# Channel attention and GELU feed-forward on one Trainium2 core: vector and scalar work in a written order, and a plain first step in each pair

## Chip, core and metric

The kernel runs on one core of a Trainium2 chip. TensorE (PE) multiplies, VectorE (DVE) and ScalarE (ACT) empty PSUM and do the elementwise work, SyncE (SP) issues the transfers. Every engine works through its own instruction stream and waits at semaphores for the others. The metric is the device time of one execution in microseconds (us); lower is better.

## What is computed

```python
B, N, C = 4, 6080, 256                          # q, k, v: (B, N, C); w_in (256, 2048), w_out (2048, 256)
qn = q / (norm(q, axis=1) + 1e-6)               # norms over the N positions of each channel
kn = k / (norm(k, axis=1) + 1e-6)
a = softmax(kn.transpose(0, 2, 1) @ qn / tau)   # 256 x 256 for each batch
x = (v @ a).reshape(24320, 256)
out = gelu(x @ w_in) @ w_out                    # exact gelu, with erf
```

## The kernel before

The attention matrix is folded into the first weight: `(v @ a) @ w_in` is `v @ (a @ w_in)`, so each batch has its own first-layer weight, which `w_part` makes in four groups `g` of 512 columns. Operands of products are kept as a high and a low fp32r half, and one product is three matmuls (high*high, high*low, low*high; `passes`).

Work is cut by batch `b` (4), by pair `p` (6 pairs of two chunks of 512 positions; the last pair, p=5, has two of 480) and by step `u` (8 steps, each with two of the sixteen 128-row blocks of the hidden layer): 192 steps in all, `steps`. A step does the first layer of its own blocks (`first_products`) and, between these, the second layer of the step before it (`second_products`, a generator that is advanced once or twice after each first-layer product). The first layer is a Strassen-Winograd scheme of seven products in the order of `ORDER`; they run in two PSUM banks, which the program calls `h` (`one` and `two` in the code, taken from a `ring`). Product 0 in `one` is copied out to SBUF by ACT (`p1`), product 1 in `two` likewise (`p5`), product 2 is accumulated in `one` and copied (`u2`); later products are added to these copies by DVE (`added`, L572), and GELU follows on ACT (L525, L526 for the high half and the whole, `whole` L535 where the scheme also covers the second layer).

Where `strassen(b, p, u)` holds, the second layer of the step also uses the scheme: four full products of 512 columns for the chunk j=1 and seven of 256 columns for chunk j=0 (into the PSUM tiles c00, c01, p0, p1), whose operands `sums` makes on DVE and ACT (x, then casts into gh1/gl1 of 768 columns, L552/L557, and gh0/gl0 of 1024, L556/L558; in the last pair 720 and 960). Where it does not, the second layer is eight full products. At the end of a pair `combine` and `merge` add p0, p1 and c00, c01 together and the result is stored.

Beside this, while batch b runs, the kernel prepares batch b+1 (`extras`): it loads tiles of q and k (`load_qk`), splits them into high and low (`split_qk`, L199 on ACT, L200 on DVE), multiplies them in bursts of eight matmuls in an `h` bank (`burst`) and adds the result to `sacc` on DVE (L218); it loads transposed tiles (raw<-kqt) and squares them on ACT for the norms (`norm_part`, L226); in the steps 36 and after of the batch it does the softmax and, from step 41, makes the next weights: `w_part` multiplies six times into an `h` bank, ACT scales the result out (hl, L437), DVE forms four sums and ACT and DVE split them into wh and wl. The values of v for the next pair are split in the last step of each pair (`v_split`, L494 and L495).

The order of instructions on each engine comes from a scheduler that orders by its own estimates of time. Only PE's instructions are held in the order in which the program writes them, from the point where "filled" is set (at the end of the first attention matrix):

```python
def pe(op, *args, **kw):
    r = op(*args, **kw)
    if "filled" in state:
        tc.keep_in_program_order(r)
    return r
```

The pair (0, 0) uses the plain form of the first layer as well (`plain_products`) while the second weight is still being narrowed from fp64; in the pair (0, 1) `sum_wo` forms the scheme's sums of the second weight once and stores them.

Of the kernel before, what the change touches and what calls it, by code (L numbers as in the profile page):

```python
# [60 lines left out]
def channel_attention_gelu_ffn(ctx, tc, qk, kqt, vt, tau, w_in, w_out, out):  # L61
# [62 lines left out]
    def pe(op, *args, **kw):  # L124
        r = op(*args, **kw)  # L125
        if "filled" in state:
            tc.keep_in_program_order(r)
        return r

    def mm(*args, **kw):  # L130
        return pe(nc.tensor.matmul, *args, **kw)
# [41 lines left out]
    def qk_fill():  # L173
        state["fill"] = s = psum("c00").rearrange("p (m c) -> p m c", m=NCT)
        for i in range(FILL * JS):
            js, j = divmod(i, JS)
            raw = raws[1, js]
            for m in range(NCT):
                marks["fill"] = nc.tensor.matmul(
# [16 lines left out]
    def split_qk(b, js):  # L196
        raw = raws.pop((b, js))
        hl = pqk.tile([P, 2, JS, 2, C], F32R, name="hl", bufs=3)
        nc.scalar.copy(out=hl[:, 0], in_=raw)  # L199
        nc.vector.tensor_tensor(out=hl[:, 1], in0=raw, in1=f32(hl[:, 0]), op=ALU.subtract)  # L200
        hls[b, js] = hl


    def burst(b, k, m):
# [7 lines left out]
        if k == 0:  # L212
            if m == 0:
                state["sacc"] = pm.tile([P, NCT, NT], F32, name="sacc")
            nc.vector.tensor_copy(out=state["sacc"][:, m], in_=s)
        else:
            acc = state["sacc"][:, m]
            nc.vector.tensor_tensor(out=acc, in0=s, in1=acc, op=ALU.add)  # L218

    def norm_part(b, t, c):  # L220
# [5 lines left out]
        nc.scalar.activation(out=x, in_=x, func=AF.Square, accum_out=state["nsum"][:, t, c:c + 1])  # L226
# [8 lines left out]
    def narrow(hi, lo, raw):  # L235
# [12 lines left out]
        nc.vector.tensor_scalar(out=top, in0=high.bitcast(F32), scalar1=TOP_MAX, scalar2=-TOP_MAX,  # L248
                                op0=ALU.min, op1=ALU.max)
        nc.scalar.activation(out=tail, in_=top, func=AF.Square)  # L250

        topu = top.bitcast(U32)
        nc.vector.tensor_scalar(out=body, in0=topu, scalar1=0x07FFFFFF, scalar2=3,
                                op0=ALU.bitwise_and, op1=ALU.logical_shift_left)
        nc.vector.scalar_tensor_tensor(out=topu, in0=topu, scalar=0xC0000000, in1=body,
                                       op0=ALU.bitwise_and, op1=ALU.bitwise_or)
        nc.vector.scalar_tensor_tensor(out=w, in0=tail, scalar=TOP_MIN ** 2, in1=top, op0=ALU.is_ge, op1=ALU.mult)

        body = high
        nc.vector.tensor_scalar(out=body, in0=w.bitcast(U32), scalar1=0xFF800000, scalar2=None, op0=ALU.bitwise_and)  # L260
        nc.vector.scalar_tensor_tensor(out=tail, in0=low, scalar=2.0 ** -52, in1=body.bitcast(F32), op0=ALU.mult,
                                       op1=ALU.mult)
        nc.scalar.copy(out=hi, in_=w)
        nc.vector.tensor_tensor(out=w, in0=w, in1=f32(hi), op=ALU.subtract)
        nc.vector.tensor_tensor(out=lo, in0=w, in1=tail, op=ALU.add)
# [30 lines left out]
    def sum_wo(u):  # L296
# [6 lines left out]
        tt = nc.vector.tensor_tensor  # L303
        tt(out=full, in0=f32(wo[:, 0]), in1=f32(wo[:, 1]), op=ALU.add)
# [3 lines left out]
        tt(out=s4, in0=a12, in1=s2, op=ALU.subtract)  # L308
        new_ws((0, 1, u))
        ws = wss.pop((0, 1, u))  # L310
        hi, lo = (ws[:, i].rearrange("p s c -> p (s c)") for i in range(2))
        nc.scalar.copy(out=hi, in_=x[:, 1])
# [4 lines left out]
    def preload(func, after):  # L317

        junk = pm.tile([P, 16], F32, name="junk")
        nc.scalar.activation(out=junk[:, 0:2], in_=after.bitcast(F32)[:, 0:2], func=func)  # L320

    def softmax(first):
# [5 lines left out]
        for m in range(NCT):  # L328
            t = pm.tile([P, C], F32, name=f"t{m}")
            if first:  # L330
                nc.scalar.copy(out=t, in_=state["s"][m])
            else:
                s = state["sacc"]
                nc.vector.tensor_tensor(out=t, in0=s[:, m, 0:C], in1=s[:, m, C:2 * C], op=ALU.add)
            ts.append(t)
        nsum = state.pop("nsum")
        if first:
# [4 lines left out]
            nc.vector.reduce_sum(out=z, in_=nsum[:, :, NSQ // NSJ:NSC], axis=AX.X)  # L342
            nc.vector.tensor_tensor(out=x, in0=nps[:, 0:2 * NCT], in1=z, op=ALU.add)
        else:
            nc.vector.reduce_sum(out=x, in_=nsum[:, :, 0:NSC], axis=AX.X)
        nc.vector.tensor_scalar(out=x, in0=x, scalar1=1e-30, scalar2=None, op0=ALU.max)
        yield

        nc.scalar.activation(out=y, in_=x, func=AF.Sqrt)
        if first:  # L350
            preload(AF.Exp, y)
        nc.vector.reciprocal(out=z, in_=y)
        nc.vector.tensor_tensor(out=z, in0=z, in1=x, op=ALU.mult)
        nc.vector.scalar_tensor_tensor(out=z, in0=z, scalar=2e-6, in1=y, op0=ALU.add, op1=ALU.add)
        nc.vector.reciprocal(out=r, in_=z)

        diag = pm.tile([P, NCT, P], F32, name="diag")
        nc.vector.tensor_tensor(out=diag, in0=ident.unsqueeze(1).broadcast_to([P, NCT, P]),
                                in1=r[:, NCT:2 * NCT].unsqueeze(2).broadcast_to([P, NCT, P]), op=ALU.mult)
        nc.vector.tensor_scalar(out=rk, in0=r[:, 0:NCT], scalar1=rtau, scalar2=4.0, op0=ALU.mult, op1=ALU.mult)  # L360
# [3 lines left out]
        for m in range(NCT):  # L364
            nc.vector.scalar_tensor_tensor(out=ts[m], in0=ts[m], scalar=rk[:, m:m + 1], in1=rq[:, 0:C],
                                           op0=ALU.mult, op1=ALU.mult)
            nc.vector.reduce_max(out=nms[:, m:m + 1], in_=ts[m], axis=AX.X, negate=True)
# [56 lines left out]
    def w_part(b, g, m):  # L424
# [19 lines left out]
        if m == 0:  # L444
            return
# [514 lines left out]
```

## Time and profile before

| | |
|---|---|
| median of 3 runs | 2304.08 us (2302.96 to 2306.28) |
| the profiled execution | 2306.74 us, its span 2305.0 us |
| mean granted TensorE clock | 0.987 |
| busy: PE, DVE, ACT | 2188.7, 1746.6, 1639.4 us |

Rows are read thus. A group of instructions has its source line, engine, operation, tiles (out<-in), shape and count, then its busy time and the mean time of one in ns, then the idle time of the engine ahead of it and what ended that. A wait row names who waited for whom: total us, times, longest. A row of a timeline has start and duration in us, and in brackets the idle time before it. A row of windows has, for a stretch of the execution, the busy time of each engine with its number of instructions, then the mean granted clock of TensorE and the DMA share. PE's busy time runs on while its last matmul drains.

### The profile page before, as it was taken

How to read it: one execution, taken by the hardware profiler on the slowest of the kernel's cores; microseconds unless marked ns; L12 is line 12 of the kernel's file. 1: busy time of each engine (PE TensorE's matmuls, PEld its weight loads, DVE VectorE, ACT ScalarE, POOL GpSimd, SP SyncE). 2: the span in 40 equal slices, each digit the busy share in tenths (PEclk: the TensorE clock that was granted, in tenths of full speed). 3: DMA queues.
4: the chain of work that ended last, by engine and by line, in shares of the span. 5: the costliest groups of instructions: out<-in, count | busy, mean ns of one | idle time of the engine just before them, and what ended most of it. 6: DMA issues, size and time to landing. Idle time of an engine off the chain costs nothing.

```text
span 2305.0 us, 30506 instructions
## 1 busy us (share of the span) xinstructions
PE 2188.7 (95%) x11239; PEld 1838.8 (80%) x11239; DVE 1746.6 (76%) x2777; ACT 1639.4 (71%) x2702; POOL 1.3 (0%) x8
## 2 busy tenths in 40 slices
PE   9899999998899999999889999999988999999998
PEld 7687788887777887788777787778877788888886
DVE  6987778877677787887767778788676787787774
ACT  6667777767567777776766777777666677777664
POOL 0000000000000000000000000000000000000000
PEclk9999999999999999999999999999999999999999
DMA  9446555434235555543324555553342332433331
GB/s 380 168 149 226 191 183 201 171 120 146 110 136 198 176 201 174 190 157 119 146 110 149 190 174 200 175 191 127 110 146 110 127 136 103 147 145 119 119 120 71
DMA packets 103429, 363.74 MB, mean 158 GB/s; under 512 B 10608, under 2 KB 12656, under 8 KB 101232
## 3 DMA queue, kind: packets, MB, share of 16 engines
q1 hardware_dynamic: 103280, 361.80, 44.3%
q8 instruction: 88, 1.44, 0.3%
q14 instruction: 61, 0.50, 0.1%
HBM read 324.27 MB, written 37.49 MB: 157 GB/s over the span
## 4 chain that ended last, share of the span: by engine, by line
PE 59%; DVE 14%; ACT 14%; DMA 8%; issue 5%; ACTq 0%; SPq 0%; DVEq 0%
PE h L125 29%; PE c L125 21%; PE p L125 7%; DMA raw<-kqt 7%; DVE h L572 3%; ACT x L535 3%; ACT raw L226 2%; DVE gl L557 2%; ACT gh L525 2%; PE h L167 2%; ACT gh L556 2%; DVE hl L200 2%; ACT g L526 2%; DVE x L549 2%; DVE gl L558 1%
## 5 line engine op out<-in xcount | busy, mean ns | idle before, releaser
L125 PE MATMUL c<-gh,wo 128*128 128x512 f32 (+3 forms) x2372 | 840.0, 362 | 0.0
L125 PE MATMUL h<-vh,wh 128*128 128x512 f32 (+1 forms) x1312 | 533.8, 407 | 99.6 <-ACT hl L437 48.8
L125 PE MATMUL h<-vl,wh 128*128 128x512 f32 (+1 forms) x1312 | 519.3, 396 | 0.0
L125 PE MATMUL h<-vh,wl 128*128 128x512 f32 (+1 forms) x1312 | 518.7, 395 | 0.0
L125 PEld LDWEIGHTS c<-gh,wo 128*128 128x128 f32 x2372 | 451.6, 190 | 76.2
L525 ACT ACTIVATE gh<-h 128x512 fp32r<-128x512 f32 (+1 forms) x402 | 250.4, 623 | 265.3 <-DVE h L572 246.9
L125 PE MATMUL c<-gl,wo 128*128 128x512 f32 (+3 forms) x1186 | 425.4, 359 | 0.0
L125 PEld LDWEIGHTS h<-vh,wh 128*128 128x128 f32 x1312 | 249.7, 190 | 183.1 <-ACT hl L437 58.5
L527 DVE TENSOR_TENSOR gl<-g,gh 128x512 fp32r<-128x512 f32 (+1 forms) x418 | 284.6, 681 | 82.6 <-ACT g L526 80.0
L558 DVE TENSOR_TENSOR gl<-x,gh 128x1024 fp32r<-128x1024 f32 (+1 forms) x175 | 211.9, 1211 | 138.3 <-ACT gh L556 138.3
L572 DVE TENSOR_TENSOR h<-h,p 128x512 f32<-128x512 f32 (+1 forms) x368 | 249.9, 681 | 64.5 <-PE h L125 56.0
L125 PEld LDWEIGHTS h<-vh,wl 128*128 128x128 f32 x1312 | 249.8, 190 | 53.7
L125 PEld LDWEIGHTS h<-vl,wh 128*128 128x128 f32 x1312 | 250.1, 191 | 31.0 <-DVE vl L495 0.3
L567 ACT COPY p<-h 128x512 f32<-128x512 f32 (+1 forms) x368 | 211.4, 580 | 80.8 <-PE h L125 80.5
L125 PEld LDWEIGHTS c<-gl,wo 128*128 128x128 f32 x1186 | 225.5, 190 | 43.1
L535 ACT ACTIVATE x<-h 128x512 f32<-128x512 f32 (+1 forms) x350 | 200.2, 603 | 65.2 <-DVE h L572 59.0
L526 ACT ACTIVATE g<-h 128x512 f32<-128x512 f32 (+1 forms) x402 | 245.2, 610 | 1.4 <-DVE h L572 1.4
L125 PE MATMUL p<-gh,ws 128*128 128x256 f32 (+1 forms) x1050 | 240.4, 280 | 0.0
L556 ACT CAST gh<-x 128x1024 fp32r<-128x1024 f32 (+1 forms) x175 | 181.8, 1039 | 78.2 <-DVE x L555 77.2
L572 DVE TENSOR_TENSOR h<-h,u 128x512 f32<-128x512 f32 (+1 forms) x184 | 125.6, 683 | 110.5 <-PE h L125 109.2
L125 PEld LDWEIGHTS p<-gh,ws 128*128 128x128 f32 x1050 | 185.9, 189 | 7.8
L549 DVE TENSOR_TENSOR x<-x 128x512 f32<-128x512 f32 (+1 forms) x175 | 119.7, 684 | 94.8 <-ACT x L535 94.5
(176 smaller groups left out, 2777.7 us busy)
## 6 DMA issues: line engine op xcount, KB each, us to landing
wo<-keep_out SPq DMA_DIRECT2D x184, 512.0 KB, 4.5
ws<-keep_sum SPq DMA_DIRECT2D x175, 512.0 KB, 3.6
raw<-qk SPq DMA_DIRECT2D x95, 512.0 KB, 4.5
raw<-kqt SPq DMA_DIRECT2D x72, 512.0 KB, 4.3
v_raw<-vt SPq DMA_DIRECT2D x20, 1024.0 KB, 6.2
out<-osb SPq DMA_DIRECT2D x40, 512.0 KB, 2.8
hl<-keep_in SPq DMA_DIRECT2D x12, 1024.0 KB, 7.4
raw<-w_in SPq DMA_DIRECT2D x8, 512.0 KB, 6.9
```

Source lines behind the costliest of these rows:

```text
L125: r = op(*args, **kw)
L167: marks["scores"] = nc.tensor.matmul(s[m], raw[:, j, 0, m * P:(m + 1) * P], raw[:, j, 1], start=(js == 0 and j == 0), stop=(js * JS + j == ...
L200: nc.vector.tensor_tensor(out=hl[:, 1], in0=raw, in1=f32(hl[:, 0]), op=ALU.subtract)
L525: nc.scalar.activation(out=gh[:, :n], in_=src, func=AF.Gelu)
L526: nc.scalar.activation(out=g[:, :n], in_=src, func=AF.Gelu)
L527: nc.vector.tensor_tensor(out=gl[:, :n], in0=g[:, :n], in1=f32(gh[:, :n]), op=ALU.subtract)
L535: nc.scalar.activation(out=state["x"][:, at:at + n], in_=src, func=AF.Gelu)
L549: tt(out=x[:, 4 * h:6 * h].rearrange("p (k c) -> p k c", k=2), in0=x[:, h:3 * h].rearrange("p (k c) -> p k c", k=2), in1=x[:, 0:h].unsquee ...
L556: nc.scalar.copy(out=ht[:, :4 * h], in_=x[:, 4 * h:8 * h])
L558: tt(out=lt[:, :4 * h], in0=x[:, 4 * h:8 * h], in1=f32(ht[:, :4 * h]), op=ALU.subtract)
L567: nc.scalar.copy(out=t[:, :n], in_=ps[:, :n])
L572: nc.vector.tensor_tensor(out=h[:, :n], in0=ps[:, :n], in1=t[:, :n], op=ALU.add)
```

## The change

Three things change.

1. From the pair (0, 1) on ("pinned"), the instructions of DVE and ACT are held in the order of the program, as PE's are. In the first pair (0, 0) PE's instructions are now left to the scheduler too.
2. The program is written slot by slot: the seven first-layer products of a step are its slots 0 to 6, `EDGE` (8) is its end. Splits, sums, squares, `v_split`, `combine`, `merge` and the softmax are cut into parts, and a table of jobs puts each part at a step and slot. The low half of a gelu is issued behind the next DVE eviction (`pending`, `flush`).
3. `strassen` is false for u=0 in every pair: the second layer of that step takes eight full products. The bursts of batches 2 and 3 come every 2.8 steps from step 4 (before: every 3 from step 2).

```diff
+    class InOrder:
...
+            def issue(*args, **kw):
+                r = op(*args, **kw)
+                if "pinned" in state:
+                    tc.keep_in_program_order(r)
+                return r
...
+    pe, dve, act = InOrder(nc.tensor), InOrder(nc.vector), InOrder(nc.scalar)
...
     def strassen(b, p, u):
-        return p > 1 if b == 0 else (b, p, u) != (B - 1, NP - 1, NU - 1)
+        return u > 0 and (b, p) > (0, 1) and (b, p, u) != (B - 1, NP - 1, NU - 1)
...
+    def flush():
+        for x in pending:
+            x()
+        pending.clear()
...
-        nc.vector.tensor_tensor(out=gl[:, :n], in0=g[:, :n], in1=f32(gh[:, :n]), op=ALU.subtract)
+        act.activation(out=gh[:, :n], in_=src, func=AF.Gelu)
+        act.activation(out=g[:, :n], in_=src, func=AF.Gelu)
+        pending.append(lambda: dve.tensor_tensor(out=gl[:, :n], in0=g[:, :n], in1=f32(gh[:, :n]), op=ALU.subtract))
...
     def sums(n):
...
-        nc.scalar.copy(out=hb[:, :3 * h], in_=x[:, h:4 * h])
-        yield
+        act.copy(out=hb[:, :3 * h], in_=x[:, h:4 * h])
         tt(out=t2, in0=t3, in1=b11, op=ALU.add)
+        yield
         tt(out=t4, in0=b21, in1=t2, op=ALU.subtract)
-        nc.scalar.copy(out=ht[:, :4 * h], in_=x[:, 4 * h:8 * h])
+        yield
+        act.copy(out=ht[:, :4 * h], in_=x[:, 4 * h:8 * h])
         tt(out=lb[:, :3 * h], in0=x[:, h:4 * h], in1=f32(hb[:, :3 * h]), op=ALU.subtract)
+        yield
         tt(out=lt[:, :4 * h], in0=x[:, 4 * h:8 * h], in1=f32(ht[:, :4 * h]), op=ALU.subtract)
...
+    def spread(gen, step, *slots):
+        for x in slots:
+            at(step + x // 10, x % 10, lambda: next(gen, None))
...
+            def split(b=b, js=js, step=prev + 1 + t):
+                gen = split_qk(b, js)
+                next(gen)
+                at(step, 2, lambda: next(gen, None))
+            at(prev + 1 + t, 1, split)
...
+            def norm(b=b, i=i, step=base + 8 + i):
+                gen = norm_part(b, *divmod(i, NSC))
+                with behind("kept"):
+                    next(gen)
+                at(step + 1, 2, lambda: next(gen, None))
+            at(base + 8 + i, EDGE, norm)
+        def soft(step=base + 36):
+            gen = softmax(False)
+            next(gen)
+            spread(gen, step, 10, 12, 10 + EDGE, 20, 23, 20 + EDGE)
...
+                spread(w_split(b, g), step, 10, 11, 12, 20, 22, 23)
...
+                    def end(b=b, p=p, step=base + NU + 1):
+                        gen = combine(b, p)
+                        next(gen)
+                        spread(gen, step, 1)
+                        for c in range(NCT):
+                            at(step, 2, lambda c=c: merge(b, p, c))
...
+        if (b, p) == (0, 1):
+            spread(sum_wo(u), i, 0, 1, 3, 4)
...
+        for slot, _ in enumerate((plain_products if plain else first_products)(b, p, u)):
+            for _ in range(1 if slot < 4 or count < 11 else 2):
+                next(second, None)
+            if slot < 2:
+                next(rest, None)
+            run(i, slot)
...
+        if mine:
+            rest = sums(PAIRS[p][1])
+            next(rest)
...
+        run(i, EDGE)
+        run(i, EDGE + 1)
+        if mine:
+            next(rest)
```

Three places show what moves. The changed kernel's DVE and ACT instructions all stand under the line of `issue`, L133.

ACT in the fourth step of the last pair of batch 0 (b=0, p=5, u=3), from the cast of the 720 columns to u2; before:

```order
L552 CAST gh_5475<-x 128x720
L556 CAST gh_5477<-x 128x960
L437 ACTIVATE hl<-h_5494,rden 128x512
L567 COPY p_5519<-h_5515 128x480
L397 CAST wh_78<-hl 128x768
L567 COPY p_5528<-h_5524 128x480
```

and now:

```order
L133 CAST gh_5428<-x 128x720
L133 ACTIVATE hl<-h_5439,rden 128x512
L133 COPY p_5452<-h_5448 128x480
L133 CAST gh_5430<-x 128x960
L133 CAST wh_78<-hl 128x768
L133 COPY p_5464<-h_5460 128x480
```

The cast of 960 columns stood ahead of the scaled eviction `hl` and of the copy p1; it now stands behind both.

ACT in a step of 512 columns with a square for the norms (b=1, p=2, u=4), before:

```order
L552 CAST gh_8416<-x 128x768
L567 COPY p_8447<-h_8443 128x512
L226 ACTIVATE raw,nsum<-raw 128x1024
L567 COPY p_8456<-h_8452 128x512
L556 CAST gh_8418<-x 128x1024
L567 COPY u_8464<-h_8443 128x512
```

and now, to the first gelu of the step:

```order
L133 COPY p_8352<-h_8348 128x512
L133 CAST gh_8324<-x 128x1024
L133 COPY p_8363<-h_8359 128x512
L133 CAST hl<-raw 128x1024
L133 COPY u_8374<-h_8348 128x512
L133 ACTIVATE raw,nsum<-raw 128x1024
L133 ACTIVATE gh<-h 128x512
```

The square of the loaded tile stood between the copies p1 and p5; it now stands behind u2, and one cast of `split_qk` between p5 and u2.

DVE in the pair (0, 1), from the last gelu halves of one step to the first eviction of the next (x<-wo is the first sum of `sum_wo`, which reads a loaded weight), before:

```order
L527 TENSOR_TENSOR gl_1711<-g,gh_1710 128x512
L527 TENSOR_TENSOR gl_1723<-g,gh_1722 128x512
L304 TENSOR_TENSOR x<-wo 128x512
L572 TENSOR_TENSOR h<-h_1762,u_1774 128x512
L305 TENSOR_TENSOR x<-x 128x128
```

and now:

```order
L133 TENSOR_TENSOR gl_1719<-g,gh_1718 128x512
L133 TENSOR_TENSOR gl_1731<-g,gh_1730 128x512
L133 TENSOR_TENSOR x<-wo 128x512
L133 TENSOR_TENSOR x<-x 128x128 x4
L133 TENSOR_TENSOR hl<-raw,hl 128x1024
L133 TENSOR_TENSOR h<-h_1759,u_1777 128x512
```

The four small sums, and in such a step the low half of a split, came behind the eviction of `two`; they now stand ahead of it.

More of the change, by code (lines that the diff above doesn't have):

```diff
@@ L605, in first_products @@
         do(6, one, False, True)
+        flush()
         chunk0(one[:, :n], 0)
         later(name)
-        if strassen(b, p, u):
-            state["sums"] = sums(n)
-            next(state["sums"])
     def plain_products(b, p, u):
@@ L641, in second_products @@
         mine = strassen(b, p, u)
-        if u == 0:
-            po.clear()
-            po["mixed"] = any(strassen(b, p, x) for x in range(NU))
-            po["plain"] = not all(strassen(b, p, x) for x in range(NU))
+        po = pos.setdefault((b, p), {})
+        mixed = any(strassen(b, p, x) for x in range(NU))
         def acc(name):
@@ L705, in second_products, with store @@
             passes(o[:, half * h:(half + 1) * h], *w, hi[:, k * h:(k + 1) * h], lo[:, k * h:(k + 1) * h], first, last)
-            if name == "c01":
-                if last:
-                    combine(b, p)
-                    if u == NU - 1:
-                        merge(b, p, 0)
-                        merge(b, p, 1)
-                        store(0, po["y"])
-            yield
+            if last and name == "c01" and u < NU - 1:
+                for _ in combine(b, p):
+                    pass
+            yield
+    def store(b, p, j, osb):
+        t0, n = PAIRS[p]
+        t = b * N + t0 + j * n
+        dst = out[:, t:t + n].rearrange("(t p) n -> p t n", p=P)
+        step = 1 if (b, p) == (B - 1, NP - 1) else NCT
+        for c in range(0, NCT, step):
+            nc.sync.dma_start(out=dst[:, c:c + step], in_=osb[:, c:c + step, :n])
     def combine(b, p):
@@ L849, in ahead, with at, run @@
             load_ws(nxt)
-    def extras(b, p, u):
-        w = p * NU + u
-        if (b, p) == (0, 0):
+    FIRSTB = FILL // NB
+    bursts = {}
+    for b in range(1, B):
+        start, num, den = (8, 5, 2) if b == 1 else (4, 14, 5)
+        for k in range(FIRSTB if b == 1 else 0, NQS // NB):
+            bursts[b, k] = (b - 1) * NP * NU + start + k * num // den
+    jobs = {}
+    def at(step, slot, job):
+        jobs.setdefault((step, slot), []).append(job)
+    def run(step, slot):
+        for job in jobs.pop((step, slot), ()):
+            job()
@@ new lines, in channel_attention_gelu_ffn @@
+    steps = [(b, p, u) for b in range(B) for p in range(NP) for u in range(NU)]
+    second, count, rest = iter(()), 0, iter(())
+    for i, (b, p, u) in enumerate(steps):
+        plain = (b, p) == (0, 0)
+        if (b, p) == (0, 1) and u == 0:
+            for name in ("p0", "p1"):
+                ring.remove(name)
+            state["pinned"] = True
+        if (b, p) == (0, 1):
+            spread(sum_wo(u), i, 0, 1, 3, 4)
+        mine = strassen(b, p, u)
+        for slot, _ in enumerate((plain_products if plain else first_products)(b, p, u)):
[4 more added lines that the diff above has]
+            run(i, slot)
+        for _ in second:
+            pass
+        run(i, 6)
+        if mine:
+            rest = sums(PAIRS[p][1])
+            next(rest)
+        if plain:
+            for _ in range(paces[u] if u < len(paces) else 0):
+                narrow_unit()
+                if units:
+                    load_unit()
+        ahead(b, p, u)
+        if plain:
```

329 lines of the change are left out of this document (158 added, 171 removed).

## The prediction

> **What bounds the kernel now.** I read the page first, then windows over stages, then PE's waits, then timelines at the places that the waits name.
>
> ```profile
> span 2305.0 us, 30506 instructions
> PE 2188.7 (95%) x11239; PEld 1838.8 (80%) x11239; DVE 1746.6 (76%) x2777; ACT 1639.4 (71%) x2702; POOL 1.3 (0%) x8
> ...
> 165.00:255.00 90.00, 88.76 (x385) 70.55 (x385) 68.89 (x125) 72.20 (x132) 0.00 (x0) 1.00 0.58 203
> 255.00:533.00 278.00, 270.81 (x1425) 227.49 (x1424) 215.92 (x334) 208.24 (x338) 0.00 (x0) 1.00 0.50 174
> 533.00:682.00 149.00, 130.58 (x660) 109.75 (x659) 108.82 (x176) 95.52 (x158) 0.00 (x0) 0.95 0.39 140
> 682.00:1100.00 418.00, 406.81 (x2143) 341.02 (x2142) 321.73 (x493) 312.23 (x508) 0.00 (x0) 1.00 0.50 172
> 1100.00:1255.00 155.00, 135.48 (x696) 113.97 (x695) 114.30 (x187) 103.28 (x173) 0.00 (x0) 0.97 0.37 134
> 1255.00:1675.00 420.00, 407.45 (x2147) 341.41 (x2146) 322.38 (x494) 312.26 (x510) 0.00 (x0) 1.00 0.48 166
> 1675.00:1828.00 153.00, 134.31 (x680) 113.20 (x679) 109.14 (x180) 99.44 (x168) 0.00 (x0) 0.96 0.34 124
> 1828.00:2205.00 377.00, 377.00 (x2019) 323.65 (x2018) 292.25 (x453) 279.71 (x454) 0.00 (x0) 1.00 0.35 128
> 2205.00:2305.00 100.00, 85.21 (x444) 73.63 (x442) 56.94 (x93) 52.96 (x91) 0.00 (x0) 0.95 0.25 93
> ```
>
> PE is the bound, and the loss is not spread evenly. In 1828 to 2205, where no next batch is prepared, PE never rests. In the four stretches around the pairs of 480 columns (533, 1100, 1675, 2205) it rests 18.42, 19.52, 18.69 and 14.79 us, 71.4 together, and its clock is below full. In the stretches of 512 columns beside a next batch it rests 1.24, 7.19, 11.19 and 12.55 us, 32.2 together.
>
> ```profile
> PE h L125 <- ACT hl L437: 48.8, 24, 2.4
> PE h L125 <- ACT p L567: 24.1, 23, 2.0
> PE h L125 <- DVE sacc L218: 8.3, 14, 1.0
> ...
> 569.78 0.80 ACT L552 CAST gh<-x 128x720 fp32r<-128x720 f32 x1
> 572.11 0.99 ACT L556 CAST gh<-x 128x960 fp32r<-128x960 f32 x1 [1.53 <-DVE x L555]
> 573.01 0.68 ACT L437 ACTIVATE hl<-h,rden 128x512 f32<-128x512 f32 x1
> 573.59 0.55 ACT L567 COPY p<-h 128x480 f32<-128x480 f32 x1
> 573.74 0.56 PE L125 MATMUL h<-vh,wh 128*128 128x480 f32 x1 [1.98 <-ACT hl L437]
> ```
>
> The waits have one pattern: PE wants an `h` bank that ACT or DVE has not emptied. The rows show why at 480 columns: ACT stood 1.53 us before the cast of 960 (it needed DVE's last sum), and behind that cast stood `hl` and p1, whose inputs were there. PE lost 1.98 us, in nearly every step of these pairs. At 512 columns the culprit is another instruction in the same place:
>
> ```profile
> 880.85 1.06 ACT L226 ACTIVATE raw<-raw 128x1024 f32<-128x1024 f32 x1 [0.85 <-DMA raw<-kqt]
> 881.82 0.18 ACT L226 ACTIVATION_READ_ACCUMULATOR raw<-raw 128x1 f32 x1
> 881.91 0.56 ACT L567 COPY p<-h 128x512 f32<-128x512 f32 x1
> 882.52 0.50 PE L125 MATMUL h<-vh,wh 128*128 128x512 f32 x1 [0.75 <-ACT p L567]
> ...
> 571.00:574.00 3.00, 1.02 (x5) 0.59 (x4) 1.89 (x3) 1.89 (x3) 0.00 (x0) 1.00 0.58 232
> 574.00:577.40 3.40, 3.40 (x10) 2.78 (x10) 3.06 (x6) 2.38 (x4) 0.00 (x0) 0.50 0.00 0
> ```
>
> The square waited 0.85 us for its transfer and held p5. The last two rows show a second price: after the wait at 571 the clock stood at 0.50 for 3.4 us, which loses 1.7 more.
>
> **The 480 pairs.** Clock: 149 x 0.05 + 155 x 0.03 + 153 x 0.04 + 100 x 0.05 = 23.2 us. With the rest of 71.4 that is 94.6. A resting PE is counted busy until its last matmul has drained (about 0.39 us, where the next would start after 0.23), so some 36 waits hide 0.16 us each, 6 more: 100.6. In the new order p1 comes before the cast of 960. From the start of product 0, in a step with `w_part`: `hl` can start at about 0.2 and ends at 0.9; p1's input is there at 0.9, p1 ends at 1.5. Product 2 needs it at four groups of 0.65, 2.6. The wait is gone with 1.1 us to spare. Then come the cast (0.99) to 2.5, one wh cast (an estimate of 0.84 to 1.05, from the L199 row below for 1024 columns) to 3.5, and p5 to 4.1, due at 3.9: at most 0.2 us, in half the steps. I keep 6 us for waits of other causes that stand now and 6 for new ones over three batches: **-88** (bounds -60 and -100).
>
> [...]
>
> **The 512 stretches beside a next batch.** They rest 32.2 us, with some 40 waits x 0.16 it is 38. The square now stands behind u2, where ACT otherwise waits for DVE; the two casts of a split, 2.00 us in one piece, are now one per step; and `sacc` on DVE no longer stands behind the low cast of 768.
>
> ```profile
> 301.57 2.00 ACT L199 CAST hl<-raw 128x1024 fp32r<-128x1024 f32 x2 [0.28 <-PE h L125]
> ...
> 721.79 0.63 ACT L525 ACTIVATE gh<-h 128x512 fp32r<-128x512 f32 x1 [1.59 <-DVE h L572]
> ...
> 1949.73 0.40 PE L125 MATMUL h<-vh,wh 128*128 128x512 f32 x1
> 1950.63 0.59 ACT L567 COPY p<-h 128x512 f32<-128x512 f32 x1 [0.29 <-PE h L125]
> ...
> 1952.50 0.39 PE L125 MATMUL h<-vh,wh 128*128 128x512 f32 x1
> ...
> 1959.82 0.40 PE L125 MATMUL h<-vh,wh 128*128 128x512 f32 x1
> ```
>
> The square takes 1.25 us (1.06 and 0.19) and the hole before the first gelu is 1.59, so it fits. The last four rows are a clean step: 10.09 us from product 0 to product 0, p1 done at 1.49 after its start, wanted by product 2 at 2.77: each copy has 1.28 us to spare. p5's input is there 1.38 later, and so on. A split between p5 and u2 takes 1.05 of u2's 1.28. But the last step of a pair now has a split, a square and four casts of v, and the step after it `combine` and `merge` ahead of an eviction. So I take 60% of 38, **-23** (bounds 0 and -38).
>
> **The plain first step.** 4 + 6 + 6 + 6 = 22 steps change 12 matmuls of 512 and 21 of 256 into 24 of 512.
>
> ```profile
> 1072.02 0.28 PE L125 MATMUL c<-gh,ws 128*128 128x256 f32 x1
> ...
> 1072.73 0.40 PE L125 MATMUL h<-vh,wh 128*128 128x512 f32 x1
> 1072.96 0.40 PE L125 MATMUL h<-vl,wh 128*128 128x512 f32 x1
> ```
>
> Starts are 0.23 us apart at 512 columns and (1072.73 - 1072.02) / 6 = 0.118 at 256. 12 x 0.23 - 21 x 0.118 = 0.28 us more PE time a step, x 22 = **+6**. It takes 3.7 us of sums and casts off DVE in that step, but in the stretch 1828 to 2205 four or five pairs began without any PE rest, so there it buys nothing. p0 and p1 are not written in that step, which gives `combine` a step more.
>
> **Softmax.** Its Sqrt and Exp now stand in ACT between the cast of 1024 and p5, one step after the other, with their table loads.
>
> ```profile
> L349 ACT ACT_TABLE_LOAD x3 | 3.8, 1283 | 0.1
> L374 ACT ACTIVATE t<-t,small 128x256 f32<-128x256 f32 x8 | 4.1, 508 | 1.7 <-DVE small L367 1.6
> ```
>
> p1 ends at 1.49, the cast at 2.54, load and Sqrt at 4.0, p5 at 4.6, due at 4.15: 0.5 late. With Exp 1.28 + 2 x 0.51 + two accumulator reads of 0.19 the block ends at 5.2: 1.65 late. 2.1 x 3 batches is 6.4, less what the softmax loses now: **+4** (0 to +6.4).
>
> **Pairs (0, 0) and (0, 1).** In (0, 0) PE follows a scheduler's estimate; the nearest row is the mean loss of the 512 stretches, 32.2 in 1206 us, which would be 3 us in 107, and the pair could gain as much at its start: 0 (-3 to +3). In (0, 1) the first sum waits for its weight:
>
> ```profile
> DVE x L304 <- DMA wo<-keep_out: 9.8, 6, 3.6
> ```
>
> That wait stays, and behind it DVE now does four small sums and in five steps a split's half (1.22 us by the next rows' kind) before it empties `two`: 5 x 0.6 = **+3** (0 to +8). Transfers move with the steps that issue them, but the queue keeps the loads of tiles ahead of the weight loads that wait for PE: 0.
>
> **Sum.** -88 - 23 + 6 + 4 + 3 = -98 on the profiled 2306.7 (span 2305.0 and 1.7 around it) is 2208.7. That execution is 2.7 above the median of 2304.1, so **2206**.
>
> **Rivals.** *New waits take the place of the old at 512 columns.* Written order cannot step aside when a transfer or DVE is late. Then the -23 is lost, softmax costs 6, and u2 behind a split is late by 0.35 us in 68 steps, +24: 2304 - 88 + 6 + 6 + 3 + 24 = 2255. For it: 1.05 of 1.28 us is used. Against: ACT has 29% to spare, and the step at 1949 carried casts of v without a rest.
>
> *Slower: the square's transfer comes too late for its slot.*
>
> ```profile
> ACT raw L226 <- DMA raw<-kqt: 45.4, 39, 3.2
> raw<-kqt SPq DMA_DIRECT2D x72, 512.0 KB, 4.3
> ```
>
> ACT now has to wait at slot 2 whatever else is ready. A load issued only as ACT arrives lands 4.3 us later; 0.34 of the hole and 1.28 of slack cover 1.6, and 72 x 2.7 = 194 us would give 2400. It passes the old time once the load lands 98 / 72 + 1.6 = 3.0 us behind the slot. The longest wait now is 3.2, the mean of the 39 is 1.2, and the load is issued at the end of the step before, some 4 to 5 us ahead, so this is unlikely. [...]
>
> *No change:* if PE's waits came from the banks' number, not from the order, nothing would move. The clean step with the same two banks speaks against it.
>
> **How the numbers follow.** Likeliest case 0.74, own range 2178 to 2232 (the bounds above, mostly of the first two terms); new waits 0.16; no change 0.02; slower 0.08. The range 2178 to 2262 holds the first two cases but for their ends. Faster by over 0.2% (about 4.6 us, what a measurement can tell) 0.89, within it 0.02, slower 0.09.
>
> **What would show it.** In the 480 pairs ACT's cast of 960 behind p1 and no PE wait of 2 us, with the clock at 1.00; the wait of PE on `hl` near nothing; a plain step of 10.3 us where it was 10.1; the square between u2 and gelu with short waits; PE late behind p5 at each softmax. I am wrong if PE waits on p or u in most steps with a split, or if ACT's waits for raw<-kqt grow well past 45 us.

## The result, and the profile after

The changed kernel takes 2178.2 us (median of 4 runs, 2176.33 to 2179.23), the kernel before 2305.18 us beside it (2302.96 to 2310.76): a ratio of 0.9445, 95% interval 0.9426 to 0.9463. The prediction was 2206, with a range from 2178 to 2262. The sign and the main mechanism held; the gain was 127 us where 98 were forecast. The median lies at the lower end of the range, and by the ratio (0.9445 of 2304.08 is 2176) the time lies 2 us under it.

The page of the changed kernel, its span and the busy time of the engines:

```profile
span 2175.4 us, 29873 instructions
PE 2149.0 (99%) x11041; PEld 1819.7 (84%) x11041; DVE 1731.9 (80%) x2710; ACT 1628.4 (75%) x2701; POOL 1.3 (0%) x8
```

PE now works 99% of the span. Before, PE's waits came to 48.8 us for `hl` and 24.1 for p; the longest groups (total, number, longest one) are now:

```profile
PE h L133 <- ACT p L133: 9.2, 9, 1.7
PE h L133 <- DVE h L133: 4.7, 15, 0.6
PE h L133 <- DMA raw<-qk: 4.2, 2, 3.6
```

The wait for `hl` has no row any more. To compare stages I cut the changed kernel's execution at the same steps as the windows of the prediction, found by the 184 copies u2, which stand once in each step from (0, 1) on. The rows are (0, 0), (0, 1), the 512 columns of batch 0, its 480 stretch, the same two for batches 1 and 2, then the two stretches of batch 3:

```profile
54.60:155.40 100.80, 99.30 (x425) 78.10 (x424) 99.81 (x199) 68.56 (x131) 0.00 (x0) 1.00 0.44 154
155.40:250.30 94.90, 91.47 (x389) 70.81 (x388) 68.48 (x125) 68.62 (x125) 0.00 (x0) 1.00 0.58 196
250.30:523.00 272.70, 269.31 (x1397) 227.53 (x1397) 216.78 (x329) 212.79 (x348) 0.00 (x0) 1.00 0.52 175
523.00:645.60 122.60, 121.69 (x640) 105.09 (x640) 99.30 (x162) 92.46 (x157) 0.00 (x0) 1.00 0.44 152
645.60:1051.10 405.50, 401.81 (x2107) 340.76 (x2106) 326.98 (x492) 315.01 (x514) 0.00 (x0) 1.00 0.52 173
1051.10:1181.00 129.90, 128.99 (x678) 111.33 (x678) 105.67 (x170) 98.27 (x167) 0.00 (x0) 1.00 0.43 147
1181.00:1587.10 406.10, 402.41 (x2109) 341.26 (x2108) 327.54 (x493) 315.36 (x515) 0.00 (x0) 1.00 0.50 168
1587.10:1714.30 127.20, 126.31 (x665) 109.20 (x664) 103.33 (x167) 95.55 (x164) 0.00 (x0) 1.00 0.42 144
1714.30:2092.50 378.20, 378.20 (x1982) 322.43 (x1981) 292.32 (x442) 275.86 (x452) 0.00 (x0) 1.00 0.35 122
2092.50:2175.40 82.90, 79.22 (x435) 70.26 (x434) 57.89 (x93) 54.04 (x94) 0.00 (x0) 1.00 0.31 106
```

The clock is 1.00 in every stage. PE rests 0.9 us in each 480 stretch of the batches 0 to 2 (before: 18.4 to 19.5), and 3.4 to 3.7 in each 512 stretch beside a next batch (before: 7.2 to 12.6); of these, 3.0 lie in the steps of softmax. Against the windows of before the lengths give:

| stretch | before | after | change | predicted |
|---|---|---|---|---|
| start and (0, 0) | 165.0 | 155.4 | -9.6 | 0 |
| (0, 1) | 90 | 94.9 | +4.9 | +3 |
| 512 beside a next batch, with softmax | 1116 | 1084.3 | -31.7 | -16 |
| 480, with the pairs' neighbours | 557 | 462.6 | -94.4 | -86 |
| 1828 to 2205 | 377 | 378.2 | +1.2 | +1 |

The predicted column puts the 6 us of the plain first steps where these lie (7 of the 22 in the 480 stretches, 11 in the 512, 4 in the last) and softmax's 4 in the 512 stretches, where its steps stand (its first Sqrt after the start comes at 406 us before the change and at 493 after). The sum, -129.6, is the difference of the spans, 2305.0 and 2175.4.

ACT in the step of 480 columns that the prediction quoted at 572 now reads thus:

```profile
555.78 0.69 ACT L133 ACTIVATE hl<-h,rden 128x512 f32<-128x512 f32 x1 [1.01 <-PE h L133]
556.43 0.56 ACT L133 COPY p<-h 128x480 f32<-128x480 f32 x1
556.89 1.00 ACT L133 CAST gh<-x 128x960 fp32r<-128x960 f32 x1
556.89 0.37 PE L133 MATMUL h<-vh,wh 128*128 128x480 f32 x1
```

`hl` and p1 come as soon as PE is done, the cast of 960 behind them, and product 1 starts at 556.89 without a wait.

### The profile page after: what moved, and what is told of

Its sections match the earlier page's. It is cut to its first block, busy times and chain, and to the rows that moved or that the text cites. A ratio compares the mean times of both kernels' runs of the same rounds, so it can differ in the third digit from the quotient of the medians.

```text
span 2175.4 us, 29873 instructions
## 1 busy us (share of the span) xinstructions
PE 2149.0 (99%) x11041; PEld 1819.7 (84%) x11041; DVE 1731.9 (80%) x2710; ACT 1628.4 (75%) x2701; POOL 1.3 (0%) x8
## 3 DMA queue, kind: packets, MB, share of 16 engines
q8 instruction: 86, 1.41, 0.3%
## 4 chain that ended last, share of the span: by engine, by line
PE 86%; DVE 7%; ACT 3%; DMA 2%; issue 1%; SPq 0%; DVEq 0%; ACTq 0%
PE h L133 44%; PE c L133 33%; PE p L133 10%; DVE vl L133 2%; DVE h L133 2%; DMA raw<-qk 1%; DVE x L133 1%; ACT gh L133 1%; DMA wo<-keep_out 1%; DVE gl L133 1%; ACT x L133 1%; DVE osb L133 0%; DMA raw<-w_in 0%; ACT g L133 0%; ACT L133 0%
## 5 line engine op out<-in xcount | busy, mean ns | idle before, releaser
L133 PE MATMUL c<-gh,wo 128*128 128x512 f32 (+3 forms) x2460 | 870.5, 364 | 0.8 <-ACT wo L133 0.8
L133 PE MATMUL h<-vh,wh 128*128 128x512 f32 (+1 forms) x1312 | 519.1, 396 | 15.9 <-ACT p L133 9.2
L133 PEld LDWEIGHTS c<-gh,wo 128*128 128x128 f32 x2460 | 462.4, 188 | 81.8 <-ACT wo L133 1.5
L133 PE MATMUL h<-vl,wh 128*128 128x512 f32 (+1 forms) x1312 | 513.4, 391 | 0.7 <-DVE vl L133 0.7
L133 PE MATMUL h<-vh,wl 128*128 128x512 f32 (+1 forms) x1312 | 513.5, 391 | 0.0
L133 ACT ACTIVATE gh<-h 128x512 fp32r<-128x512 f32 (+1 forms) x446 | 278.1, 624 | 229.8 <-DVE h L133 217.6
L133 PE MATMUL c<-gl,wo 128*128 128x512 f32 (+3 forms) x1230 | 443.7, 361 | 0.0
L133 DVE TENSOR_TENSOR gl<-x,gh 128x768 fp32r<-128x768 f32 (+3 forms) x306 | 329.6, 1077 | 64.0 <-ACT gh L133 63.9
L133 DVE TENSOR_TENSOR gl<-g,gh 128x512 fp32r<-128x512 f32 (+1 forms) x462 | 313.9, 680 | 37.7 <-ACT g L133 35.7
L133 DVE TENSOR_TENSOR h<-h,p 128x512 f32<-128x512 f32 (+1 forms) x368 | 251.0, 682 | 79.2 <-PE h L133 67.0
L133 ACT COPY p<-h 128x512 f32<-128x512 f32 (+1 forms) x368 | 213.5, 580 | 131.9 <-PE h L133 131.2
L133 PEld LDWEIGHTS h<-vh,wh 128*128 128x128 f32 x1312 | 247.0, 188 | 72.5 <-ACT p L133 14.0
L133 ACT CAST gh<-x 128x768 fp32r<-128x768 f32 (+3 forms) x306 | 286.9, 937 | 12.4 <-DVE x L133 7.9
L133 DVE TENSOR_TENSOR x<-x 128x256 f32<-128x256 f32 (+4 forms) x491 | 241.3, 494 | 67.3 <-ACT x L133 49.9
L133 PEld LDWEIGHTS h<-vh,wl 128*128 128x128 f32 x1312 | 246.3, 188 | 51.6
L133 PEld LDWEIGHTS h<-vl,wh 128*128 128x128 f32 x1312 | 246.7, 188 | 36.9 <-DVE vl L133 1.1
L133 ACT ACTIVATE g<-h 128x512 f32<-128x512 f32 (+1 forms) x446 | 272.0, 610 | 0.0
L133 PEld LDWEIGHTS c<-gl,wo 128*128 128x128 f32 x1230 | 231.0, 188 | 44.7
L133 ACT ACTIVATE x<-h 128x512 f32<-128x512 f32 (+1 forms) x306 | 180.6, 608 | 48.7 <-DVE h L133 47.6
L133 PE MATMUL p<-gh,ws 128*128 128x256 f32 (+1 forms) x918 | 210.2, 280 | 0.0
L133 DVE TENSOR_TENSOR h<-h,u 128x512 f32<-128x512 f32 (+1 forms) x184 | 125.6, 683 | 89.5 <-PE h L133 88.7
L133 PEld LDWEIGHTS p<-gh,ws 128*128 128x128 f32 x918 | 162.6, 189 | 6.8
```

## The experiments

Times below are medians; a version's cost against the changed kernel is given as the difference of spans of profiled executions (2175.4 for the changed kernel), since these differ by little from run to run (2174.3 to 2177.2 in its four). A difference of under 3 us in the whole span says nothing by itself; the lengths of single pairs repeat far better (the pair (3, 1) takes 81.07 to 81.09 us in ten of the versions).

### What holds the order, and what writes it

One run keeps the new text and holds PE alone in order; one keeps the old text and holds all three engines.

```diff
 # pe_only, in the changed kernel
-                if "pinned" in state:
+                if "pinned" in state and self.engine is nc.tensor:
 # old_pinned, in the kernel before, from (0, 1) on, for nc.vector and nc.scalar
+    dve, act = InOrder(nc.vector), InOrder(nc.scalar)
```

> The changed kernel with only PE held in program order from pair (0, 1) on; ACT and DVE are left to the scheduler, the program's text stays slot by slot. If the gain comes from the fixed order on ACT and DVE: the casts of 960 and the squares go back ahead of p1 and p5, PE waits for ACT and DVE of 50 us or more come back, and the time is 2230 to 2310. Rival, the new writing order does it by itself (the scheduler follows the program closely once each job stands at its slot): 2175 to 2190, and PE's waits as in the changed kernel.

> The kernel before with ACT and DVE held in its own program order from pair (0, 1) on, nothing else changed. There, squares, splits, softmax and w_part stand together at the end of a step and the cast of 1024 or 960 behind them, all ahead of the next p1. If the slots matter, pins alone gain nothing: p1 behind all of it, 2300 to 2450. Rival, the pins matter and not the slots: below 2230.

pe_only took 2256.03 us (ratio 0.9778, 0.9764 to 0.9793), old_pinned 3030.59 (1.3128, 1.3106 to 1.315), far above what was expected. PE's waits, first those of pe_only, then of old_pinned:

```profile
PE h L133 <- ACT hl L133: 36.1, 18, 2.5
PE h L133 <- ACT p L133: 15.9, 18, 2.0
```

```profile
PE h L142 <- ACT p L85: 401.7, 168, 6.6
PE h L142 <- DVE h L85: 112.6, 198, 1.1
```

Neither half does it alone. With ACT and DVE free, the new text keeps 52 of the 130 us; the wait for `hl` is back and 78 us are lost. With the old text held as written, p1 stands behind a step's whole side work and PE loses 2.4 us (401.7 / 168) at each wait. A held order is as good as the text that it holds.

### The pairs of 480 columns: one chain through two engines

cast_early puts only ACT's cast of 960 back ahead of `hl` and p1; low720_ahead adds DVE's low cast of 720 ahead of the last sum; gelu_low_ahead adds the low half of the second gelu ahead of the last eviction. All three in the pairs of 480 columns alone.

```diff
 # cast_early: the sums' remaining parts at the end of the step, ahead of w_part
             next(rest)
+            if p == NP - 1:
+                next(rest)
+                next(rest)
 # low720_ahead: in sums, for n < NT
+            tt(out=lb[:, :3 * h], in0=x[:, h:4 * h], in1=f32(hb[:, :3 * h]), op=ALU.subtract)
             tt(out=t4, in0=b21, in1=t2, op=ALU.subtract)
 # gelu_low_ahead: in first_products
         do(5, two, True, True)
+        if n < NT:
+            flush()
```

> The changed kernel with one edit in the pairs of 480 columns: the cast of 960 columns (with the low cast of 720 on DVE) is written at the end of the step, ahead of hl and p1, as it stood before. If this one place made the loss of the 480 pairs: PE waits of about 2 us for hl and p1 come back in most of the 32 steps, the clock falls to 0.50 behind them, and the time rises by 60 to 94 us, to 2238 to 2272. Rival, the cast was late only because DVE's sums were late, and DVE's written order has mended that: the cast no longer waits, p1 comes 1 us late at most, and the time rises by less than 25 us.

> The changed kernel with two of the old places in the pairs of 480 columns: ACT's cast of 960 ahead of hl and p1 (as in the run cast_early, which cost 11 us), and DVE's low cast of 720 (0.90 us) ahead of its last sum t4, so that the cast of 960 gets its input 0.9 us later. Theory now: the old wait is a chain through both engines, last eviction, x, sums, cast of 960, hl, p1, and each early link on DVE adds its own length once the slack is gone. cast_early leaves PE 0.2 to 0.5 us of wait a step, so 0.9 more in some 28 steps is 25 us and little of the clock: 2205 to 2235. Rival, ACT's order alone made the old loss and cast_early's 11 us is all of it: 2187 to 2195.

> The run low720_ahead with one more old place in the same pairs: DVE subtracts the low half of the second gelu (0.66 us, and its wait for ACT) ahead of the eviction of product 5 instead of behind it, so that x, the sums and the cast of 960 all come about 1.1 us later. By the chain theory all three links of the old order are then back, PE waits about 2 us a step for hl and the clock falls behind it: 60 to 90 us above the changed kernel, 2238 to 2270. Rival (something else in the old kernel, the place of w_part's sums or of combine, made the rest): below 2225.

| version | median us | ratio to before | the four 480 pairs, us |
|---|---|---|---|
| before | 2305.18 | 1 | 426.1 |
| changed | 2178.2 | 0.9445 (0.9426 to 0.9463) | 343.4 |
| cast_early | 2189.61 | 0.9487 (0.9473 to 0.9501) | 354.5 |
| low720_ahead | 2209.4 | 0.9588 (0.957 to 0.9605) | 373.7 |
| gelu_low_ahead | 2255.16 | 0.9785 (0.9761 to 0.9808) | 421.7 |

Three old places bring back 78.3 of the 82.7 us that these pairs had gained (their lengths from u2 of the first step to u2 of the next pair's first, of the last pair to the end). The first alone costs 11, where 60 to 94 were expected: the rival held. The second costs 19 more, the third 48 more. In cast_early the cast waits 0.84 us, and PE 0.21:

```profile
553.31 1.00 ACT L133 CAST gh<-x 128x960 fp32r<-128x960 f32 x1 [0.84 <-DVE x L133]
554.21 0.68 ACT L133 ACTIVATE hl<-h,rden 128x512 f32<-128x512 f32 x1
554.95 0.48 PE L133 MATMUL h<-vh,wh 128*128 128x480 f32 x1 [0.21 <-ACT hl L133]
```

Before the change DVE had the two places that the other versions restore: the gelu's low half ahead of the eviction, and the low cast of 720 ahead of the last sum. From the step that the prediction quoted:

```profile
567.37 0.66 DVE L527 TENSOR_TENSOR gl<-g,gh 128x480 fp32r<-128x480 f32 x1 [0.33 <-ACT g L526]
567.94 0.65 DVE L572 TENSOR_TENSOR h<-h,p 128x480 f32<-128x480 f32 x1
...
570.80 0.90 DVE L557 TENSOR_TENSOR gl<-x,gh 128x720 fp32r<-128x720 f32 x1
571.62 0.40 DVE L555 TENSOR_TENSOR x<-x 128x240 f32<-128x240 f32 x1
```

In gelu_low_ahead the chain can be read from end to end, and ACT's wait for DVE's sum is the very 1.53 us of before:

```profile
595.66 0.66 DVE L133 TENSOR_TENSOR gl<-g,gh 128x480 fp32r<-128x480 f32 x1 [0.58 <-ACT g L133]
596.24 0.65 DVE L133 TENSOR_TENSOR h<-h,p 128x480 f32<-128x480 f32 x1
596.92 1.06 ACT L133 ACTIVATE x<-h 128x480 f32<-128x480 f32 x2 [1.29 <-DVE h L133]
...
599.04 0.90 DVE L133 TENSOR_TENSOR gl<-x,gh 128x720 fp32r<-128x720 f32 x1
599.86 0.40 DVE L133 TENSOR_TENSOR x<-x 128x240 f32<-128x240 f32 x1
600.35 0.99 ACT L133 CAST gh<-x 128x960 fp32r<-128x960 f32 x1 [1.53 <-DVE x L133]
601.25 0.68 ACT L133 ACTIVATE hl<-h,rden 128x512 f32<-128x512 f32 x1
601.98 0.52 PE L133 MATMUL h<-vh,wh 128*128 128x480 f32 x1 [1.82 <-ACT hl L133]
```

The low half (0.66, with 0.58 of waiting) holds the eviction, that holds x and the sums, the low cast of 720 (0.90) holds the last sum, that holds the cast of 960, and behind this stand `hl` and p1, for which PE waits.

### One engine held

```diff
 # act_free: nc.scalar is left out; dve_free: nc.vector is left out
-                if "pinned" in state:
+                if "pinned" in state and self.engine is not nc.scalar:
```

> The changed kernel with PE and DVE held in program order and ACT left to the scheduler. By the chain theory DVE's order carries most of the 480 pairs: these stay within 4 us a pair of the changed kernel, and the time is 2180 to 2215. Rival, ACT's order carries it: 2235 to 2260, as with neither held (2256).

> The changed kernel with PE and ACT held in program order and DVE left to the scheduler. By the chain theory the links on DVE come back, but ACT's p1 no longer stands behind the cast of 960, so that PE does not wait for the sums in the 480 pairs; held ACT meets late DVE results elsewhere: 2185 to 2225. Rival, one free engine is as bad as two: 2245 to 2265.

act_free took 2204.27 us (0.9564, 0.9545 to 0.9583), dve_free 2222.12 (0.9641, 0.9624 to 0.9659). The four 480 pairs take 357.3 and 355.1 us. With both engines free (pe_only) they take 408.9, with both held 343.4: the new text alone saves 17 us against the 426.1 of before, and of the 65.5 us that the held order adds, DVE's by itself brings 52 and ACT's by itself 54. A step of act_free, then one of dve_free:

```profile
572.73 1.00 ACT L133 CAST gh<-x 128x960 fp32r<-128x960 f32 x1 [0.84 <-DVE x L133]
573.63 0.68 ACT L133 ACTIVATE hl<-h,rden 128x512 f32<-128x512 f32 x1
```

```profile
579.72 0.69 ACT L133 ACTIVATE hl<-h,rden 128x512 f32<-128x512 f32 x1
...
580.37 0.56 ACT L133 COPY p<-h 128x480 f32<-128x480 f32 x1
580.74 0.40 DVE L133 TENSOR_TENSOR x<-x 128x240 f32<-128x240 f32 x1
581.17 1.00 ACT L133 CAST gh<-x 128x960 fp32r<-128x960 f32 x1 [0.24 <-DVE x L133]
```

In act_free the cast stands ahead of `hl`, but DVE's sum is early. In dve_free DVE's sum is late (its low cast of 720 stands ahead of it), but `hl` and p1 do not stand behind the cast. The chain needs both ends in their old order; cutting either removes most of it. Most of what the second held engine adds in dve_free lies in the 512 columns: there the clean pairs (3, 1) to (3, 3) take 83.3 to 83.5 us in dve_free and 81.07 with DVE held.

### The 512 columns

```diff
 # square_old_place: square between p1 and p5, cast of 1024 behind p5 in the steps with a square
-                at(step + 1, 2, lambda: next(gen, None))
+                at(step + 1, 0, lambda: next(gen, None))
 # sacc_behind_low: in sums, in steps with a burst, ahead of sacc and the last sum
+        if early:
+            tt(out=lb[:, :3 * h], in0=x[:, h:4 * h], in1=f32(hb[:, :3 * h]), op=ALU.subtract)
```

> The changed kernel with the 72 squares of the norms back at the old place on ACT, between p1 and p5, and the cast of 1024 behind p5 in the same steps, as before the change. p5 has 1.28 us to spare and the square takes 1.25, so only what the square then waits for its transfer and what else is late reaches PE: if the square made most of the loss at 512 columns, 0.2 to 0.5 us in each of 72 steps, 14 to 36 us slower, 2192 to 2214. Rival, it is DVE's lateness that made those waits too and the square's place costs under 5 us: 2176 to 2183.

> The changed kernel with DVE's low cast of 768 (0.95 us) ahead of the addition to sacc in all 68 steps with a burst, and so ahead of the last sum too, as it often stood before. In the changed kernel DVE waits 0.7 us for the burst there, so sacc comes 0.3 us later, which its bank can bear, and the cast of 1024 about 1 us later: if nothing else is late, under 5 us, 2177 to 2183. Rival, as the prediction had it, sacc behind this cast makes a good part of the loss at 512 columns: 8 to 20 us, 2186 to 2198.

square_old_place took 2195.19 us (0.9525, 0.9511 to 0.954): 17.8 us more span, 0.25 us for each of the 72 squares. That is a little under half of the 39 us that the order gained in the 512 stretches (31.7, with 11 x 0.31 = 3.4 for the plain steps and 3.8 for softmax, both of which lie in them). PE now waits for the copy u2, a wait that the changed kernel shows in no row of PE:

```profile
PE h L133 <- ACT u L133: 5.5, 11, 0.7
```

sacc_behind_low took 2182.85 us (0.9471, 0.9456 to 0.9487): 4.4 us more span. The low cast of 768 ahead of `sacc` is a small part. The remaining 17 us of the 512 stretches, if the parts add up at all, were not taken apart; the casts of a split in one piece, which the prediction named, were not tested.

### The first pair

```diff
-                if "pinned" in state:
+                if "pinned" in state or self.engine is nc.tensor and "filled" in state:
```

> The changed kernel with PE held in program order in the pair (0, 0) as well, as before the change. Before, PE waited 2.6, 2.3 and 3.1 us there for the halves of w_in that DVE was still narrowing; if the scheduler's freedom to put other products first removed these waits, they come back and the clock with them: 6 to 12 us slower, 2184 to 2190. Rival, DVE's and ACT's work of that pair is ahead because it is written otherwise: no change, within 3 us of 2178.

2187.47 us (0.9489, 0.9475 to 0.9503), 10.9 us more span, and all of it in (0, 0): the first u2 of (0, 1) comes at 170.4 instead of 159.7 us (before: 169.5), and no later pair differs by over 0.1 us. In the runs that leave (0, 0) as it is this copy came between 158.7 and 162.0, so the figure is good to 2 or 3 us. The window of this pair before the change, then PE's wait in it, then the same wait in this run:

```profile
58.00:165.00 107.00, 99.05 (x413) 78.26 (x411) 98.60 (x191) 68.54 (x129) 0.00 (x0) 0.95 0.42 147
```

```profile
PE p L125 <- DVE hl L265: 4.9, 2, 2.5
```

```profile
PE p L133 <- DVE hl L133: 4.9, 2, 2.5
```

The waits are the same to a tenth, and so is a third, of 2.1 us, for the half that ACT narrows. Held in order, PE must stand still until DVE has narrowed a half of w_in; left to the scheduler, it does other products first.

### The plain first step

```diff
 # scheme_u0, scheme_u0_early
-        return u > 0 and (b, p) > (0, 1) and (b, p, u) != (B - 1, NP - 1, NU - 1)
+        return (b, p) > (0, 1) and (b, p, u) != (B - 1, NP - 1, NU - 1)
 # scheme_u0_early alone: combine in the first step, both merges in the next step's slot 0
-                    at(base + NU + 1, 0, end)
+                    at(base + NU, 6, end)
```

> The changed kernel with the scheme in the first step of each pair too (c01's second half alone is merged, as before the change, where no step of a pair is plain). If the plain step only costs PE time: 0.31 us less in each of 22 steps, 6.9 us faster, 2171. Rival, the plain step makes room for merge, combine and v's casts: without it the sums of that step and the store of the last pair come together on DVE, and each of 21 pairs loses 0.5 us or more, 2181 to 2200.

> The run scheme_u0 with combine back at the end of the pair's first step and the merges at the first slot of the second, ahead of the sums' low halves, about where they stood before the change. If the place of combine made that run's 15 us, PE's waits for the merge (8.7 us) go, and with 0.31 us less PE time in each of 22 steps it ends near or below the changed kernel: 2168 to 2180. Rival, the first step needs the room that the plain form gives DVE (no sums beside combine, merge and the casts of v): 2186 to 2200.

scheme_u0 took 2193.97 us (0.9509, 0.9495 to 0.9523), scheme_u0_early 2188.78 (0.9487, 0.9473 to 0.9501): 17.2 and 12.2 us more span. Both were expected to end near or below the changed kernel; in both the rival held. The 480 pairs take 345.8 and 346.5 us in them, so the plain step is not what these pairs gained by. PE's waits in the one, then in the other:

```profile
PE h L133 <- DVE h L133: 13.4, 23, 1.1
PE c L133 <- DVE osb L133: 8.7, 14, 1.0
```

```profile
PE h L133 <- ACT p L133: 19.8, 26, 1.7
```

With combine and merge late, the merge and the evictions behind it on DVE hold PE; with them early, the wait for the merge is gone and ACT's p1 and p5 are late instead. The pairs (3, 1) to (3, 3) show the price alone: 80.75 us before the change (scheme in each step, order by the scheduler), 81.07 changed, 81.55 and 81.79 in these runs. The plain step costs the 0.31 us of PE time that was forecast, and the scheme costs more than that in both written orders tried. That a third order would reach 80.75 is likely from the row of before, and was not tried.

### A faster version

```diff
 # ACT and DVE held from (0, 2) on; Sqrt behind p5; Exp behind u2, its table loaded ahead of p1;
 # the last sum of the two softmax steps ahead of softmax's work on DVE
-            spread(gen, step, 10, 12, 10 + EDGE, 20, 23, 20 + EDGE)
+            spread(gen, step, 11, 12, 10 + EDGE, 22, 23, 20 + EDGE)
+            preload(AF.Exp, ident)
+        early = mine and i % (NP * NU) in (36, 37)
+        if early:
+            next(rest)
         run(i, EDGE)
```

> A version meant to be faster than the changed kernel: in (0, 1) ACT and DVE are left to the scheduler (there the run with both free was 5 us shorter); Sqrt stands behind p5, not ahead of it; the last sum of the two softmax steps stands ahead of softmax's own DVE work; Exp's table is loaded ahead of p1 by an activation of 2 columns and the two Exp stand behind u2. Softmax costs PE three times 1.18 + 0.40 + 1.88 us in the changed kernel: if these places make it, some 9 us of 10.4 go, and 4 to 5 in (0, 1): 2163 to 2168. Rival, the load moves its lateness to the gelus and the next step: only (0, 1) is gained, 2172 to 2176.

> softmax_moved (2166) with the scheme in the first step and combine and merge at the early places as in scheme_u0_early. If these places make the scheme free there, 6 us faster, 2158 to 2163; by the rival, 8 to 20 us slower, 2174 to 2186. The two runs should differ by the 12 us that softmax_moved gained.

softmax_moved took 2165.97 us (0.9396, 0.9382 to 0.941): faster than both kernels. The changed kernel's row at the Sqrt shows what was there to gain, the table load and Sqrt ahead of p5, and PE behind p5:

```profile
491.72 1.28 ACT L133 ACT_TABLE_LOAD   x1
493.01 0.20 ACT L133 ACTIVATE small<-small 128x4 f32<-128x4 f32 x1
493.13 0.57 ACT L133 COPY p<-h 128x512 f32<-128x512 f32 x1
...
493.75 0.51 PE L133 MATMUL h<-vh,wh 128*128 128x512 f32 x1 [1.01 <-ACT p L133]
```

The wait of PE for p falls from 9.2 us to this:

```profile
PE h L133 <- ACT p L133: 1.0, 3, 0.3
```

The pairs (0, 4), (1, 4) and (2, 4) are 2.2 us shorter each, 6.5 in all where 9 were expected (waits for DVE's t grew from 0.7 to 3.1 us), and (0, 1) is 5.9 shorter. softmax_moved_u0 took 2178.48 us (0.9442, 0.9426 to 0.9458): the early combine is no better on this base (the rival again), and it lies 10.3 below scheme_u0_early, about the 12 that the two bases differ by.

## Why the prediction held in kind and fell short in size

The mechanism was right: the order on ACT and DVE was the loss, and the 480 pairs were most of it. What failed was the size of three terms: 512 columns above all, then (0, 0) and 480 columns.

- **512 columns, -23: the largest error.** The step "So I take 60% of 38" failed. The stretches are 31.7 us shorter although the plain steps (3.4) and softmax (3.8) made them longer, so the order was worth 39 us there, 16 more than the term. The new waits for which the 40% came off did not come: outside softmax PE rests 0.4 to 0.7 us a stretch. The bound of 38 comes out about right, but not by its parts. PE's busy time in the three stretches fell from 1085.1 to 1073.5 us although the plain steps added 3.4, so 15 us of the loss had stood in time that the profile counts as busy, where the prediction put 40 x 0.16 = 6. Of the causes named, the square's place is worth 17.8 and `sacc` behind the low cast 4.4.
- **480 columns, -88: the mechanism held, the size was too small.** The step "I keep 6 us for waits of other causes that stand now and 6 for new ones" failed: PE rests 0.9 us in each of the first three stretches, so hardly anything was to be kept. With the 7 plain steps taken out (2.2), the stretches gained 96.6 of the 100.6 that the rows gave. The named cause, `hl` and p1 behind the cast of 960, is one end of a chain; with ACT's order alone 54 of 65.5 us are there. The other end, DVE's late sum, is as good (52 with DVE's order alone). The quoted row had it: ACT stood 1.53 us "before the cast of 960 (it needed DVE's last sum)". The prediction asked what stood behind the cast, and not why the sum was late.
- **(0, 0), 0 (-3 to +3): wrong.** The step "the nearest row is the mean loss of the 512 stretches" took a far row where the stage had its own: 99.05 busy in 107 us and a clock of 0.95, a loss of 8.0 + 5.4 = 13 us. That PE was freed there was in the diff. It was worth 9.6, and first_pair_held gives 10.9 back.
- **Plain first step, +6: right.** 0.31 us a pair in the clean pairs, where 0.28 was worked out. That it buys DVE room was dismissed from the stretch 1828 to 2205 of before; in the written order it does buy something, 12 to 17 us against the two versions without it.
- **Softmax, +4: right in sum, by luck.** PE's starts stand 1.41 us apart at Sqrt, 0.63 at the bank of the softmax product and 2.11 at Exp, where 0.23 is usual: 1.18, 0.40 and 1.88 late, 3.46 a batch where 2.1 was worked out. The last sum was late as well, so p5 stood behind a late cast, too. The steps u=4 to 7 of pair 4 grew by 2.7 us a batch, 8.1 in all (one burst less in the batches 1 and 2, 1.4 us, is counted in). But what softmax lost before was more than the 2.4 that the term took off. Sqrt stood in pair 3 then, its table load and gelu's (1.28 us each) ahead of the gelus, and behind these PE waited 1.13, 1.58 and 1.59 us for x, 4.3 together, which is gone: 3.8 in all.
- **(0, 1), +3: right in kind, 4.9.** Released again, the pair is 5.9 shorter.
- **The rivals.** New waits at 512 columns did not come; ACT's waits for raw<-kqt, 45.4 us before, have no row any more, so the slower case had no footing; the no-change case fell with the 480 pairs.
- **The range.** Beyond their terms the order at 512 columns gave -15.9, (0, 0) -9.6 and the order at 480 columns -8.6; softmax came out 0.2 lower, (0, 1) took 1.9 more and the plain steps 0.8. Together these are the 31.6 us by which the sum missed. The lower end, 2178, was drawn from the first two terms' bounds "mostly"; the sum of all lower bounds (-100 - 38 + 6 + 0 + 0 - 3 = -135) would have put it at 2169.

## What to carry to other kernels

Where an engine waits, follow the chain past the first culprit: an instruction that holds a queue while it waits for another engine has two cures, and either can do (here 54 and 52 of 65.5 us). A bound that is worked out from rows of rest and clock is worth more than a discount from it for troubles that no row shows, and each stage's own row comes before a mean over others. Holding an order pays only together with the text that spells it out: the new text alone gave 0.978, held it gave 0.9445, and the old text held gave 1.31.

## What the runs showed of the hardware

The granted clock was lower in the versions with the most waits of PE for `hl` and p, but it did not fall behind each long rest. In the profiled executions these waits come to 9.2 us in the changed kernel, 14.8 in cast_early and 33.7 in low720_ahead, with a mean clock of 1.000 in all three; to 52.0 in pe_only and 59.8 in gelu_low_ahead (0.992 in both), to 72.9 before (0.987, and 16 falls to half in the trace) and to 402.6 in old_pinned (0.931). Two stretches of gelu_low_ahead stand each behind a rest of about 2 us. In the first rest PE stood still for 2.14 us (2.90 - 0.76), and the 3.3 us behind it ran at 1.00; in the second it was 1.82 us (3.30 - 1.48), and the 3.4 us behind it had a mean clock of 0.54:

```profile
586.10:589.00 2.90, 0.76 (x5) 0.33 (x3) 1.79 (x4) 1.67 (x3) 0.00 (x0) 1.00 0.58 222
589.00:592.30 3.30, 3.30 (x15) 2.89 (x16) 1.95 (x5) 2.12 (x4) 0.00 (x0) 1.00 0.00 0
...
598.70:602.00 3.30, 1.48 (x8) 0.95 (x6) 2.17 (x4) 1.77 (x4) 0.00 (x0) 1.00 0.73 289
602.00:605.40 3.40, 3.40 (x9) 2.88 (x10) 1.40 (x2) 1.88 (x3) 0.00 (x0) 0.54 0.00 0
```

The longer of the two rests left the clock whole, so the length of a rest does not tell by itself what follows it; what decides it was not shown.

The clock gives a good part of the size of the chain's third step. In low720_ahead the waits for `hl` and p have means of 1.0 and 1.1 us (20.6 us in 21, 13.1 in 12) and the mean clock is 1.000; in gelu_low_ahead they have means of 1.9 and 1.6 us (40.9 in 21, 18.9 in 12), and the clock of 0.992 costs some 0.008 x 2255 = 18 us more, an estimate. The waits grew by 26 us (33.7 to 59.8), which with these 18 makes 44 of the third step's 48.
